# Three first expert passes in plain float32, the first interleaved with the last unit, in a fused scan, feed-forward and routing kernel

## Chip, cores and metric

The kernel runs on one core of one Trainium2 chip. The metric is the device time of one execution in microseconds (us), lower is better. The engines are PE (TensorE, matrix products), ACT (ScalarE), DVE (VectorE), POOL (GpSimd) and SP (SyncE, which here only issues transfers). Each executes its instructions in the order in which they were written.

## What is computed

Three stages follow one another; 3,072 tokens have 256 channels each.

```python
# 1: a chunked scan per head gives x of 3072 x 256
# 2: a feed-forward layer with a rational activation
h = x @ w_in                                   # 256 -> 2048
P = a[0] + a[1]*h + a[2]*h**2 + a[3]*h**3
Q = 1 + abs(b[0])*abs(h) + abs(b[1])*h**2
x = (P / (Q + 1e-6)) @ w_out                   # 2048 -> 256
# 3: each token goes to one of 8 experts
logits = normalized(x) @ normalized(expert_emb).T / tau
e = argmax(logits); gate = softmax(logits)[e]
out = gate * (relu(x @ w1[e]) @ w2[e])         # 256 -> 1024 -> 256
```

## The kernel before

All work is written into a planner (class `Plan`): every instruction has an engine, an estimated duration and a key `at`, and `Plan.run` simulates the engines and starts, on each free engine, the ready instruction with the lowest key. The order so found is the order of the instructions on each engine's queue. Buffers with the same tag (SBUF tiles and PSUM banks) are given out strictly in the order of the first key of their users. Keys count blocks of stage 2: block i of unit u has the key 16u + i.

Stages 1 and 2 run together in six units of 512 tokens, each of 16 blocks of 128 hidden channels (`block`). A block has six products on PE into a bank of four (tag `h`, L735), then five ACT instructions (L740, L741, L742, L746, L747), four on DVE (L744, L749, L750, L751), one on POOL (L752, `gl`), and six products on PE into the unit's two accumulator banks (`acc`, L761). Values on both sides of a product are split into a high and a low float32r part, and three float32r products stand for one float32 product. Unit 5, the last, has no stage 1 beside it.

After a unit, `unit_out` (L773) brings the accumulators to SBUF as x2T, and `route` transposes the rows and computes logits (L794, L796, copies L799 into `row`), finds the expert and the slot in a chain of small DVE instructions (L813 to L850) with one small product (`rk`), and scatters the rows into the table `xs` by four indirect transfers on POOL (L853). After unit 4, `rank` sorts the eight experts by their tokens so far (L873 to L889) and loads the eight numbers into registers of SP (L892), so that the weights of "the expert of rank r" can be fetched.

Stage 3 is a list of passes (rank, first tile, tiles of 128 tokens). FIRST, `(0, 0, [2])` and `(1, 0, [2])`, needs only the tokens of units 0 to 4; THEN needs unit 5's too. Each change of expert loads eight pieces of 256 KB, four of w1 and four of w2 (L941, raw buffers of tag `raw`, four of them), which `weights` splits: high part on ACT (L942), low part by a subtraction on DVE or POOL (L945), into tags `eah`, `eal`, `ebh`, `ebl` with six buffers each. `tokens` fetches rows from `xs` (L956), transposes them (L964) and splits them (L967, L970); `gate` computes the factor (L985 to L1003); `hidden` has six products (L1018) into an `h` bank, a relu split in two (L1020, L1021) and three products for each tile (L1027) into banks of tag `acc`; `deliver` scales (L1041, L1043) and scatters the rows to the output (L1047, POOL). The pool of the fetched rows opens only when all of unit 5's first products are issued (`open_sp`); the pool `w3` of the weights takes the memory of stage 1 (`open_w3`).

Of the kernel before, what the change touches and what calls it, by code (L numbers as in the profile page):

```python
# [17 lines left out]
P = 128  # L18
# [8 lines left out]
TPE = 4  # L27
# [1 line left out]
ROW = DM + NE + 1  # L29


FIRST = [(0, 0, [2]), (1, 0, [2])]
THEN = [(0, 2, [2]), (1, 2, [2])] + [(r, 0, [3]) for r in range(4, NE)] + [(2, 0, [4]), (3, 0, [2, 2])]

WIDE = 4
LATE = 1

SOON = 0.0
EARLY = sum(FIRST[0][2])
assert all(f == (r, 0, [EARLY]) for r, f in enumerate(FIRST))  # L40

# [11 lines left out]
def sh(at, late, early):  # L53

    return at + (early if at < 4 else late)
# [16 lines left out]
class Plan:  # L72
# [29 lines left out]
    def op(self, eng, us, at, fn, r=(), w=(), lag=0.0, size=0, after=(), port=None):  # L102

        port = {None: ("POOL",), True: ("POOL", "DVE"), False: ()}[port]
        o = dict(port=port, on=eng if isinstance(eng, dict) else {eng: us}, any=isinstance(eng, dict), at=at, fn=fn, lag=lag, size=size, i=len(self.ops))
        deps = set()  # L110
        vals = {}
        for x, wr in [(x, False) for x in r] + [(x, True) for x in w]:
            v, s = x if isinstance(x, tuple) else (x, None)
            vals[id(v)] = v
            hit = lambda z: z[1] is None or s is None or z[1] == s
            deps.update(z[0] for z in v.wr if hit(z))
            if wr:
                deps.update(z[0] for z in v.rd if hit(z))
        for x, wr in [(x, False) for x in r] + [(x, True) for x in w]:
            v, s = x if isinstance(x, tuple) else (x, None)  # L120
            if wr:
                if s is None:
# [150 lines left out]
def ssm_ffn_moe_kernel(  # L273
# [54 lines left out]
    def big(shape, dt, name):  # L328
        return plan.val(blk, shape, dt, name, "big", BIG)
# [533 lines left out]
    def rank(s):  # L863

        l0 = (NG - LATE) * BU // P
        v = lambda shape, k, dt=F32: plan.val(blk, shape, dt, f"r{k}", f"r{k}", 1)
        sm, key, rk8, se = v([P, NE], "sm", BF16), v([P, NE], "key"), v([P, NE], "rk8"), v([P, NE, NE], "se")
        cn = bank("cn")
        rows_, cols_ = (lambda ap: ap[:, :, None].to_broadcast([P, NE, NE])), (lambda ap: ap[:, None, :].to_broadcast([P, NE, NE]))

        def f():
            with nc.allow_low_precision(reason="whole numbers below 256"):
                V.tensor_reduce(out=sm.t, in_=oh[:, 0:l0].rearrange("p c e -> p e c"), op=ALU.add, axis=AX.X)  # L873
        dv = lambda us, fn, r, w: op("DVE", us, s, fn, r=r, w=w)
        dv(0.08 + l0 * NE / 960, f, [(oh, u) for u in range(NG - LATE)], [sm])
        op("PE", 0.06, s, lambda: T.matmul(out=cn[:, 0:NE], lhsT=ones.t, rhs=sm.t, start=True, stop=True), r=[ones, sm], w=[cn])

        dv(0.1, lambda: V.scalar_tensor_tensor(out=key.t, in0=cn[:, 0:NE], scalar=float(NE), in1=cw8.t, op0=ALU.mult, op1=ALU.add), [cn, cw8], [key])
        dv(0.15, lambda: V.tensor_tensor(out=se.t, in0=cols_(key), in1=rows_(key), op=ALU.is_gt), [key], [se])
        dv(0.15, lambda: V.tensor_reduce(out=rk8.t, in_=se.t, op=ALU.add, axis=AX.X), [se], [rk8])  # L880

        dv(0.08, lambda: V.tensor_scalar(out=kmin.t, in0=rk8.t, scalar1=float(len(FIRST)), scalar2=float(EARLY * P), op0=ALU.is_lt, op1=ALU.mult), [rk8], [kmin])
        dv(0.08, lambda: V.tensor_scalar(out=tcap.t, in0=rk8.t, scalar1=float(WIDE), scalar2=float(TPE - 1), op0=ALU.is_lt, op1=ALU.add), [rk8], [tcap])

        dv(0.08, lambda: V.tensor_scalar(out=rk8.t, in0=rk8.t, scalar1=-1.0, scalar2=float(NE), op0=ALU.mult, op1=ALU.add), [rk8], [rk8])
        dv(0.15, lambda: V.tensor_tensor(out=se.t, in0=cols_(rk8), in1=rows_(cw8), op=ALU.is_equal), [rk8, cw8], [se])
        dv(0.15, lambda: V.tensor_tensor(out=se.t, in0=se.t, in1=cols_(cw8), op=ALU.mult), [se, cw8], [se])
        dv(0.15, lambda: V.tensor_reduce(out=key.t, in_=se.t, op=ALU.add, axis=AX.X), [se], [key])
        dv(0.08, lambda: V.tensor_scalar(out=slot.t, in0=key.t, scalar1=-1.0, scalar2=float(NE), op0=ALU.mult, op1=ALU.add), [key], [slot])  # L889

        def f():
            _, e = nc.values_load_multi_w_load_instructions(slot[0:1, :], engines=[mybir.EngineType.SP], min_val=0, max_val=NE - 1)  # L892
            expert.extend(e)
        op("SP", 1.0, s, f, r=[slot], w=[ranked])


    def s1_unit(u, lo, hi):
# [32 lines left out]
    def weights(e, i, at, nm):  # L930

        half, q = i % 2, i // 2
        k = "ab"[half]
        shape = [P, 2, 256]
        raw = plan.val(w3, shape, F32, f"r{k}{nm}_{q}", "raw", 4)
        hi, lo = (plan.val(w3, shape, FR, f"e{k}{z}{nm}_{q}", f"e{k}{z}", 6) for z in "hl")
        if half == 0:
            src = lambda: w1[bass.ds(expert[e], 1), :, q * 256:(q + 1) * 256].rearrange("o (k p) f -> p (o k) f", p=P)
        else:
            src = lambda: w2[bass.ds(expert[e], 1), q * 256:(q + 1) * 256, :].rearrange("o (k p) d -> p (o k) d", p=P)  # L940
        op("SP", 0.47, sh(at - 6, -0.52, 0), lambda: D(out=raw.t, in_=src()), r=[one, ranked], w=[raw], size=262144)  # L941
        op("ACT", acts(512), sh(at, 1.69, 0), lambda: A.activation(out=hi.t, in_=raw.t, func=AF.Copy), r=[raw], w=[hi])  # L942
        op(
            {"DVE": dve(512), "POOL": pool2(512)}, 0, sh(at, 7.77, 0),
            lambda g: (G if g == "POOL" else V).tensor_tensor(out=lo.t, in0=raw.t, in1=hi.t.bitcast(F32), op=ALU.subtract),  # L945
            r=[raw, hi], w=[lo], port=True,
        )
        ew[e, k, q] = hi, lo
# [104 lines left out]
    def run_pass(e, t0, parts, at):  # L1053
# [5 lines left out]
        for n in parts:  # L1059
# [15 lines left out]
    for u in range(NBU):  # L1075
        if u + 1 < NBU:
            for v in range(2):
                s1_unit(2 * u + 2 + v, NF * u + 8 * v - 0.5, NF * u + 8 * v + 6.0)
        for i in range(NF):
            block(u, i, NF * u + i)  # L1080
            if u == 0 and i % 2:
                clear(i // 2, 8.0 + i, [last_of[u, i]])
        unit_out(u, NF * (u + 1) + 2 - (SOON if u >= NG - LATE else 0))
        if u < NG - LATE:
            route(u, NF * (u + 1) + 2)
        if u == NG - LATE - 1:
            rank(NF * (u + 1) + 4)
    op("X", 0.0, sh(S3 - 12, 4.15, 0), open_w3, w=[one], after=plan.users(s1p))
    op("X", 0.0, S3 - 2, open_sp, w=[two], after=plan.users(wi))
    at = S3  # L1090
    held = None
    for j, (e, t0, parts) in enumerate(FIRST + THEN):
        if j == len(FIRST):
            for g in range(NG - LATE, NG):
                route(g, NF * (g + 1) + 2)
            at += 4
        if e != held:
            for i in range(8):
# [318 lines left out]
```

## Time and profile before

| | |
|---|---|
| median of 3 runs | 615.38 us (614.1 to 615.79) |
| the profiled execution | 620.6 us, of it the span from first to last instruction 618.8 us |
| PE busy | 551.9 us (89% of the span) |
| DVE busy | 485.5 us (78%) |
| ACT busy | 481.2 us (78%) |
| POOL busy | 258.3 us (42%) |
| granted TensorE clock, mean | 0.957 of full speed |

Shares are means over the span; the stages have different limits, so the rows below are by stretch. Matmuls are pipelined and their durations overlap in the records: what a product costs in a dense stretch is the distance from one start to the next.

### The profile page before, as it was taken

To read this page: it belongs to the slowest core of one execution; us is meant where nothing else is said; L and a number is where in the kernel's file an instruction comes from. 1 tells how busy PE (TensorE), PEld (TensorE's weight loads), DVE (VectorE), ACT (ScalarE), POOL (GpSimd) and SP (SyncE) were. 2 spreads that over 40 slices of the span, in tenths; PEclk is the share of its full clock that TensorE was granted. 3 is DMA by queue.
4 is the path that set the end of the run, shared out by engine and by line. 5 is a ranking of instruction groups with operands and counts; after the bars stand their busy time and mean duration, and the time that the engine had idled before them with its cause. 6 is when DMAs were issued, how large, how long until landed. Compare 5 with 4: busy or idle time off the path is not lost.

```text
span 618.8 us, 10551 instructions
## 1 busy us (share of the span) xinstructions
PE 551.9 (89%) x3477; PEld 428.3 (69%) x3477; DVE 485.5 (78%) x990; ACT 481.2 (78%) x967; POOL 258.3 (42%) x240
## 2 busy tenths in 40 slices
PE   1578989999999999999999998558989999999991
PEld 0144757676676677767766786346979989998991
DVE  7998899899887999899879889477577777766430
ACT  6899989999997999989979997766677656565320
POOL 2573434445445444454454336852456230212111
PEclk9858999999999999999999999768999999999997
DMA  7960606022102110210020012431676655552000
GB/s 249 391 186 19 184 19 183 4 80 73 37 17 93 39 44 32 82 36 1 1 71 2 0 37 86 137 86 35 190 228 188 193 144 155 180 176 76 18 29 14
DMA packets 45728, 58.99 MB, mean 95 GB/s; under 512 B 3991, under 2 KB 35584, under 8 KB 45664
## 3 DMA queue, kind: packets, MB, share of 16 engines
q1 hardware_dynamic: 43168, 51.82, 27.7%
q0 software_dynamic: 2496, 6.41, 2.9%
q8 instruction: 29, 0.48, 0.3%
q14 instruction: 35, 0.29, 0.2%
HBM read 44.02 MB, written 14.72 MB: 95 GB/s over the span
## 4 chain that ended last, share of the span: by engine, by line
PE 55%; issue 13%; DVE 7%; ACT 6%; DMA 5%; POOL 4%; SPq 1%; another core or an unknown queue 0%; POOLq 0%; ACTq 0%
PE acc L761 19%; PE h L735 19%; PE eh L1018 4%; PE y L1027 3%; PE c L663 3%; PE y L703 2%; DMA ra<-in_w 2%; POOL out_dram L1047 2%; PE y L709 2%; PE tk L796 1%; DMA g<-xs 1%; ACT p L740 1%; ACT v L746 1%; DVE u L750 1%; PE st L685 1%
## 5 line engine op out<-in xcount | busy, mean ns | idle before, releaser
L752 POOL TENSOR_TENSOR gl<-p,v 128x512 fp32r<-128x512 f32 x96 | 128.0, 1335 | 169.8 <-DVE p L751 75.8
L735 PE MATMUL h<-x1h,wiw 128*128 128x512 f32 x384 | 144.7, 421 | 19.6 <-DVE p L751 17.3
L761 PE MATMUL acc<-gh,wow 128*128 128x512 f32 x384 | 113.0, 417 | 0.0
L735 PEld LDWEIGHTS h<-x1h,wiw 128*128 128x128 f32 x384 | 75.2, 196 | 47.1 <-DVE p L751 19.6
L761 PEld LDWEIGHTS acc<-gh,wow 128*128 128x128 f32 x384 | 69.6, 193 | 30.1 <-issue 15.9
L749 DVE SCALAR_TENSOR_TENSOR gh<-h,as,v 128x512 fp32r<-128x512 f32 x96 | 71.7, 747 | 21.5 <-ACT v L747 18.8
L744 DVE SCALAR_TENSOR_TENSOR h<-p,sl,h 128x512 f32<-128x512 f32 x96 | 71.8, 749 | 13.1 <-ACT v L741 12.8
L750 DVE SCALAR_TENSOR_TENSOR u<-u,lq,gh 128x512 f32<-128x512 f32 x96 | 80.4, 838 | 0.8
L735 PE MATMUL h<-x1l,wiw 128*128 128x512 f32 x192 | 78.5, 409 | 0.0
L740 ACT ACTIVATE p<-h,kk 128x512 f32<-128x512 f32 x96 | 65.2, 679 | 16.2 <-POOL gl L752 11.3
L751 DVE SCALAR_TENSOR_TENSOR p<-h,as,u 128x512 f32<-128x512 f32 x96 | 71.4, 744 | 3.1 <-issue 0.2
L742 ACT ACTIVATE u<-v,qb 128x512 f32<-128x512 f32 x96 | 69.6, 725 | 1.6
L746 ACT ACTIVATE v<-u,lq 128x512 f32<-128x512 f32 x96 | 69.4, 723 | 1.6
L1027 PE MATMUL y<-ebh,hh 128*128 128x256 f32 x224 | 65.0, 290 | 1.5 <-DVE yo L1043 0.8
L1027 PE MATMUL y<-ebh,hl 128*128 128x256 f32 x224 | 64.1, 286 | 1.9 <-DVE hl L1021 1.5
L1021 DVE SCALAR_TENSOR_TENSOR hl<-eh,hh 128x256 fp32r<-128x256 f32 (+2 forms) x88 | 42.8, 492 | 28.4 <-ACT hh L1020 27.6
L1027 PE MATMUL y<-ebl,hh 128*128 128x256 f32 x224 | 63.3, 282 | 0.0
L1047 POOL DMA_INDIRECT out_dram<-yo,g x28 | 29.0, 1036 | 81.2 <-DVE yo L1043 62.3
L761 PE MATMUL acc<-gl,wow 128*128 128x512 f32 x192 | 61.2, 400 | 1.3 <-POOL gl L752 1.2
L747 ACT ACTIVATE v<-v 128x512 f32<-128x512 f32 x96 | 60.4, 630 | 1.0
L1020 ACT ACTIVATE hh<-eh 128x256 fp32r<-128x256 f32 (+2 forms) x88 | 38.1, 435 | 26.8 <-PE eh L1018 23.9
L741 ACT ACTIVATE v<-h 128x512 f32<-128x512 f32 x96 | 56.9, 593 | 2.5 <-POOL gl L752 2.5
(222 smaller groups left out, 1138.8 us busy)
## 6 DMA issues: line engine op xcount, KB each, us to landing
ra<-in_w SPq DMA_DIRECT2D x40, 256.0 KB
rb<-in_w SPq DMA_DIRECT2D x40, 256.0 KB
xb<-in_xb SPq DMA_DIRECT2D x12, 384.0 KB
xs<-empty SPq DMA_DIRECT2D x8, 530.0 KB
wiwr<-in_w_in SPq DMA_DIRECT2D x8, 512.0 KB
wowr<-in_w_out SPq DMA_DIRECT2D x8, 512.0 KB
xrow<-row SPq DMA_DIRECT2D x6, 530.0 KB
bc<-in_bct SPq DMA_DIRECT2D x12, 256.0 KB
```

What stands on the lines that cost most here:

```text
L735: T.matmul(out=h.t, lhsT=part(wiw[g_], z)[:, k, fs], rhs=xx[:, k, :], start=(k == 0 and e == 0), stop=(k == 1 and e == 2))
L740: op("ACT", act(512, 1), s, lambda: A.activation(out=pp.t, in_=h.t, func=AF.Square, bias=kk.t), r=[h, kk], w=[pp])
L742: op("ACT", acts(512) + 0.06, s + 0.3, lambda: A.activation(out=uu.t, in_=vv.t, func=AF.Square, bias=qb.t), r=[vv, qb], w=[uu])
L744: op("DVE", dve(512, 1), s + 0.8, lambda: stt(out=h.t, in0=pp.t, scalar=sl.t, in1=h.t, op0=ALU.add, op1=ALU.mult), r=[h, pp, sl], w=[h])
L746: op("ACT", acts(512) + 0.09, s + 0.9, lambda: A.activation(out=vv.t, in_=uu.t, func=AF.Ln, bias=lq.t), r=[uu, lq], w=[vv])
L747: op("ACT", acts(512), s + 1.0, lambda: A.activation(out=vv.t, in_=vv.t, func=AF.Exp, scale=-1.0), r=[vv], w=[vv])
L749: op("DVE", dve(512, 1), s + 1.5, lambda: stt(out=gh.t, in0=h.t, scalar=as_.t, in1=vv.t, op0=ALU.add, op1=ALU.mult), r=[h, as_, vv], w=[gh])
L750: op("DVE", dve(512, 1), s + 1.6, lambda: stt(out=uu.t, in0=uu.t, scalar=lq.t, in1=gh.t.bitcast(F32), op0=ALU.add, op1=ALU.mult), r=[uu, l ...
L751: op("DVE", dve(512, 1), s + 1.7, lambda: stt(out=pp.t, in0=h.t, scalar=as_.t, in1=uu.t, op0=ALU.add, op1=ALU.subtract), r=[h, as_, uu], w ...
L752: op("POOL", pool2(512), s + 2.1, lambda: G.tensor_tensor(out=gl.t, in0=pp.t, in1=vv.t, op=ALU.mult), r=[pp, vv], w=[gl])
L761: T.matmul(out=acc[dh].t, lhsT=part(wow[g_], z)[:, i % 2, dh * P:(dh + 1) * P], rhs=x.t, skip_group_check=True, start=(i == 0 and e == 0), ...
L1027: T.matmul(out=y[t // 2][:, t % 2 * DM:(t % 2 + 1) * DM], lhsT=hx[:, o], rhs=wb[w][:, f % 2, :], start=(f == 0 and i == 0 and t % 2 == 0), ...
```

## The change

FIRST becomes three passes, of the experts of ranks 0, 1 and 2; rank 2's pass of four tiles in THEN shrinks to its last two. A new function `first_pass` does them with plain float32 products: the eight weight pieces land unsplit in the `eah`, `eal`, `ebh`, `ebl` buffers, the rows in a `raw` buffer (widened from 512 to 530 words), the transposes go through one bank, the relu is one instruction on ACT or DVE, and one product stands where three float32r products stood. The first of them (`SMALL = 1`) has keys from 92 in steps of 1.2, so it lies among unit 5's last blocks, and its output bank is one of the two small `s` banks; the others follow at key 99 with output in an `acc` bank. Unit 4's `unit_out`, `route` and `rank` get keys that are lower by `AHEAD = 4`; `open_w3` gets key 80; the planner's estimate of the register load is 2.0 in place of 1.0.

```diff
-FIRST = [(0, 0, [2]), (1, 0, [2])]
-THEN = [(0, 2, [2]), (1, 2, [2])] + [(r, 0, [3]) for r in range(4, NE)] + [(2, 0, [4]), (3, 0, [2, 2])]
+FIRST = [(0, 0, [2]), (1, 0, [2]), (2, 0, [2])]
+THEN = [(0, 2, [2]), (1, 2, [2]), (2, 2, [2])] + [(r, 0, [3]) for r in range(4, NE)] + [(3, 0, [2, 2])]
+AHEAD = 4.0
+SMALL = 1
@@ route
+        elif u == NG - LATE - 1:
+            s -= AHEAD
@@ rank
-        op("SP", 1.0, s, f, r=[slot], w=[ranked])
+        op("SP", 2.0, s, f, r=[slot], w=[ranked])
@@ weights
-        raw = plan.val(w3, shape, F32, f"r{k}{nm}_{q}", "raw", 4)
+        raw = plan.val(w3, [P, 2, ROW], F32, f"r{k}{nm}_{q}", "raw", 4)
@@ new
+    def first_pass(e, n, load, at, step, small):
...
+            w = wt[half, q] = plan.val(w3, [P, 2, 256], F32, f"f{k}{nm}_{q}", f"e{k}{'hl'[q % 2]}", 6)
+            op("SP", 0.47, load + 0.1 * i, lambda half=half, q=q, w=w: D(out=w.t, in_=src_of(e, half, q)), r=[one, ranked], w=[w], size=262144)
+        g = plan.val(w3, [P, 2, ROW], F32, f"fg{nm}", "raw", 4)
+        x = plan.val(w3, [P, 2, n * P], F32, f"fx{nm}", "hl", 3)
...
+        tr = bank(f"ft{nm}")
...
+        op("ACT", act(2 * n * P), at - 1.5, lambda: A.activation(out=x.t.rearrange("p k t -> p (k t)"), in_=tr[:, 0:2 * n * P], func=AF.Copy), r=[tr], w=[x])
+        gt = gate(plan, nm, g, n, at + 4 * step, blk)
+        y = bank(f"fy{nm}") if small else plan.val(ps_a, [P, 512], F32, f"fy{nm}", "acc", 2, True)
+        m = n * P
+        for c in range(8):
...
+                for k in range(2):
+                    T.matmul(out=h[:, 0:m], lhsT=wa[:, k, c % 2 * P:(c % 2 + 1) * P], rhs=x[:, k, :], start=(k == 0), stop=(k == 1))
...
+                for t in range(n):
+                    T.matmul(
+                        out=y[:, t * DM:(t + 1) * DM], lhsT=hh[:, t * P:(t + 1) * P], rhs=wb[:, c % 2, :],
...
+            ac = at + step * c
+            op("PE", 0.45 * n, ac - 1, mm1, r=[x, wa], w=[h])
+            op({"ACT": act(m), "DVE": dve(m)}, 0, ac - 18.4, relu, r=[h], w=[hh])
+            op("PE", 0.45 * n, ac + 0.8, mm2, r=[hh, wb], w=[y])
+        deliver(nm, 0, n, g, [y], gt, at + 8 * step + 0.9)
@@ the main list
-        unit_out(u, NF * (u + 1) + 2 - (SOON if u >= NG - LATE else 0))
+        unit_out(u, NF * (u + 1) + 2 - (SOON if u >= NG - LATE else AHEAD if u == NG - LATE - 1 else 0))
-            rank(NF * (u + 1) + 4)
-    op("X", 0.0, sh(S3 - 12, 4.15, 0), open_w3, w=[one], after=plan.users(s1p))
+            rank(NF * (u + 1) + 4 - AHEAD)
+    op("X", 0.0, NF * (NG - 1), open_w3, w=[one], after=plan.users(s1p))
+        if j < len(FIRST):
+            first_pass(e, EARLY, NF * (NG - 1) + 2 + 2 * j, 92.0 if j < SMALL else at, 1.2 if j < SMALL else 0.5, j < SMALL)
+            at += 2 * EARLY if j >= SMALL else 0
+            continue
```

## Rows read from the trace of the kernel before

**Rows 1.** The page's 40 equal slices of the span: busy tenths of PE

```profile
PE   1578989999999999999999998558989999999991
```

**Rows 2.** Busy time by stretch: length, then PE, PEld, DVE, ACT, POOL, clock, DMA

```profile
377.60:391.80 14.20, 10.89 (x43) 7.60 (x42) 11.63 (x16) 10.56 (x20) 8.95 (x8) 1.00 0.32 104
391.80:416.00 24.20, 11.47 (x30) 8.73 (x30) 13.17 (x17) 16.24 (x29) 19.15 (x15) 0.65 0.47 131
416.00:429.40 13.40, 10.48 (x43) 8.21 (x42) 11.74 (x36) 7.93 (x24) 4.18 (x3) 0.87 0.13 41
429.40:459.20 29.80, 27.92 (x230) 26.30 (x228) 17.19 (x49) 19.81 (x53) 12.79 (x11) 1.00 0.62 183
459.20:606.20 147.00, 143.13 (x1051) 138.77 (x1051) 93.94 (x251) 82.01 (x217) 37.44 (x34) 1.00 0.43 129
```

**Rows 3.** Timeline of PE: start, us, instruction, idle before it and what ended it

```profile
398.07 0.80 PE L735 MATMUL h<-x1h,wiw 128*128 128x512 f32 x1 [6.25 <-DVE p L751]
409.30 0.80 PE L735 MATMUL h<-x1h,wiw 128*128 128x512 f32 x1 [6.48 <-DVE p L751]
```

**Rows 4.** Timeline of ACT

```profile
370.97 0.67 ACT L740 ACTIVATE p<-h,kk 128x512 f32<-128x512 f32 x1
374.07 0.67 ACT L740 ACTIVATE p<-h,kk 128x512 f32<-128x512 f32 x1
381.49 0.69 ACT L740 ACTIVATE p<-h,kk 128x512 f32<-128x512 f32 x1 [3.57 <-POOL gl L752]
410.70 0.69 ACT L740 ACTIVATE p<-h,kk 128x512 f32<-128x512 f32 x1 [4.67 <-POOL gl L752]
429.41 1.27 ACT L773 ACTIVATE x2T<-acc,fin 128x512 f32<-128x512 f32 x2 [1.45 <-PE acc L761]
```

**Rows 5.** Groups of 377.6 to 429.4, shapes apart: busy us, mean ns, idle before

```profile
L945 POOL TENSOR_TENSOR eal<-ra,eah 128x512 fp32r<-128x512 f32 x6 | 8.0, 1349 | 0.3 <-ACT eah L942 0.3
L942 ACT ACTIVATE eah<-ra 128x512 fp32r<-128x512 f32 x6 | 3.8, 632 | 1.6 <-DMA ra<-in_w 1.4
L1020 ACT ACTIVATE hh<-eh 128x256 fp32r<-128x256 f32 x1 | 0.4, 383 | 0.6 <-PE eh L1018 0.6
```

**Rows 6.** Timelines of DVE and SP: routing chain, ranks, first weight piece fetched

```profile
366.67 0.18 DVE L813 TENSOR_REDUCE mx<-row 128x4 f32<-128x32 f32 x1
379.44 0.16 DVE L889 TENSOR_SCALAR slot<-rkey 128x8 int32<-128x8 f32 x1
...
382.93 0.40 SPq L941 DMA_DIRECT2D ra<-in_w  x1
```

**Rows 7.** Busy time of L735, then L761, in unit 5's rest

```profile
377.60:429.40 51.80, 12.86 (x37) 8.38 (x36) 0.80 0.34 100
377.60:429.40 51.80, 19.70 (x66) 14.29 (x66) 0.80 0.34 100
```

**Rows 8.** Chain that ended last, dense runs of products: start, us to next piece

```profile
367.30 1.40 PE acc L761 x6
431.95 0.35 PE tk L796 x4
435.74 0.71 PE eh L1018 x6
436.44 0.72 PE y L1027 x6
```

**Rows 9.** Weight loads of a plain float32 product, 512 columns on the moving side

```profile
321.84 0.29 PEld L663 LDWEIGHTS c<-cz,bc 64*128 64x128 f32 x2 [0.36 <-issue]
322.73 0.29 PEld L663 LDWEIGHTS c<-cz,bc 64*128 64x128 f32 x2 [0.59 <-DVE x1l L720]
```

**Rows 10.** From unit 5's end to THEN: rows fetched (SP, chain), first product (PE)

```profile
450.09 4.71 DMA g<-xs
459.25 0.39 PE L1018 MATMUL eh<-xl,eah 128*128 128x256 f32 x1 [0.37 <-DVE xl L970]
```

**Rows 11.** Waits of SP's queue from 380 to 606: total, times, longest

```profile
SPq L941 <- DVE eal L945: 29.2, 11, 14.9
```

More of the change, by code (lines that the diff above doesn't have):

```diff
@@ L940, in weights @@
             src = lambda: w2[bass.ds(expert[e], 1), q * 256:(q + 1) * 256, :].rearrange("o (k p) d -> p (o k) d", p=P)
-        op("SP", 0.47, sh(at - 6, -0.52, 0), lambda: D(out=raw.t, in_=src()), r=[one, ranked], w=[raw], size=262144)
-        op("ACT", acts(512), sh(at, 1.69, 0), lambda: A.activation(out=hi.t, in_=raw.t, func=AF.Copy), r=[raw], w=[hi])
+        op("SP", 0.47, sh(at - 6, -0.52, 0), lambda: D(out=raw[:, :, 0:256], in_=src()), r=[one, ranked], w=[raw], size=262144)
+        op("ACT", acts(512), sh(at, 1.69, 0), lambda: A.activation(out=hi.t, in_=raw[:, :, 0:256], func=AF.Copy), r=[raw], w=[hi])
         op(
             {"DVE": dve(512), "POOL": pool2(512)}, 0, sh(at, 7.77, 0),
-            lambda g: (G if g == "POOL" else V).tensor_tensor(out=lo.t, in0=raw.t, in1=hi.t.bitcast(F32), op=ALU.subtract),
+            lambda g: (G if g == "POOL" else V).tensor_tensor(out=lo.t, in0=raw[:, :, 0:256], in1=hi.t.bitcast(F32), op=ALU.subtract),
             r=[raw, hi], w=[lo], port=True,
@@ L1066, in run_pass, with src_of, f, mm1 @@
             q += n
+    def src_of(e, half, q):
+        if half == 0:
+            return w1[bass.ds(expert[e], 1), :, q * 256:(q + 1) * 256].rearrange("o (k p) f -> p (o k) f", p=P)
+        return w2[bass.ds(expert[e], 1), q * 256:(q + 1) * 256, :].rearrange("o (k p) d -> p (o k) d", p=P)
+    def first_pass(e, n, load, at, step, small):
+        nm = f"{e}_0"
+        wt = {}
+        for i in range(8):
+            half, q = i % 2, i // 2
+            k = "ab"[half]
+            w = wt[half, q] = plan.val(w3, [P, 2, 256], F32, f"f{k}{nm}_{q}", f"e{k}{'hl'[q % 2]}", 6)
+            op("SP", 0.47, load + 0.1 * i, lambda half=half, q=q, w=w: D(out=w.t, in_=src_of(e, half, q)), r=[one, ranked], w=[w], size=262144)
+        g = plan.val(w3, [P, 2, ROW], F32, f"fg{nm}", "raw", 4)
+        x = plan.val(w3, [P, 2, n * P], F32, f"fx{nm}", "hl", 3)
+        op("SP", 0.47, load - 0.1, lambda: D(out=g.t, in_=xs[bass.ds(expert[e] * CAP, n * P), :].rearrange("(t p) c -> p t c", p=P)), r=[xs_v, xs_c, one, ranked], w=[g], size=n * P * ROW * 4)
+        tr = bank(f"ft{nm}")
+        def f():
+            for t in range(n):
+                for k in range(2):
+                    T.transpose(out=tr[:, (k * n + t) * P:(k * n + t + 1) * P], in_=g[:, t, k * P:(k + 1) * P], identity=ident.t)
+        op("PE", 0.22 * n, at - 1.5, f, r=[g, ident], w=[tr])
+        op("ACT", act(2 * n * P), at - 1.5, lambda: A.activation(out=x.t.rearrange("p k t -> p (k t)"), in_=tr[:, 0:2 * n * P], func=AF.Copy), r=[tr], w=[x])
[3 more added lines that the diff above has]
+        for c in range(8):
+            h = plan.val(ps_h, [P, 512], F32, f"fh{nm}_{c}", "h", H_B, True)
+            hh = plan.val(w3, [P, TPE * P], F32, f"fr{nm}_{c}", "hh", 3)
+            wa, wb = wt[0, c // 2], wt[1, c // 2]
+            def mm1(h=h, wa=wa, c=c):
+                for k in range(2):
+                    T.matmul(out=h[:, 0:m], lhsT=wa[:, k, c % 2 * P:(c % 2 + 1) * P], rhs=x[:, k, :], start=(k == 0), stop=(k == 1))
+            def relu(eng, h=h, hh=hh):
+                if eng == "ACT":
+                    A.activation(out=hh[:, 0:m], in_=h[:, 0:m], func=AF.Relu)
+                else:
+                    V.tensor_scalar(out=hh[:, 0:m], in0=h[:, 0:m], scalar1=0.0, scalar2=None, op0=ALU.max)
+            def mm2(hh=hh, wb=wb, c=c):
+                for t in range(n):
+                    T.matmul(
+                        out=y[:, t * DM:(t + 1) * DM], lhsT=hh[:, t * P:(t + 1) * P], rhs=wb[:, c % 2, :],
+                        start=(c == 0 and t == 0), stop=(c == 7), skip_group_check=True,
+                    )
+            ac = at + step * c
[3 more added lines that the diff above has]
+        deliver(nm, 0, n, g, [y], gt, at + 8 * step + 0.9)
```

## Prediction

> **What bounds the kernel now.** I read the page's slices first. PE is busy nine tenths or more nearly everywhere, and there is one hole, four slices (8, 5, 5, 8) from 371 to 433 us [rows 1]. So the end is set by PE's work plus what PE loses, and the loss sits where stage 2 hands over to stage 3. The windows by stretch put numbers on it [rows 2]. From 391.8 to 416.0 PE is busy 11.47 of 24.20 us at a mean granted clock of 0.65, so part of that work ran at the lower level, 1.2 GHz, and took double; from 459.2 to 606.2 it is busy 143.13 of 147.00 at full clock. After 606.2 there are 12.6 us of tail that the change does not touch.
>
> What makes the hole: PE stands for 6.25 and 6.48 us before two first products of unit 5's blocks, which lack a free bank because the DVE work of earlier blocks is late [rows 3]. DVE was late for ACT, and ACT for POOL: ACT idles 4.67 us for `gl` before the block at 410.70 [rows 4]. POOL was splitting the weights of the first expert at 1349 ns a piece (six of `eal`, as many of `ebl`), in order ahead of unit 5's `gl`; ACT splits six pieces of each kind too, at 632 ns, and waited there for the transfers [rows 5]. So the first pass's preparation, not its products, held unit 5 up. Unit 5 ends with x2T at 429.41 [rows 4]; from there its routing has to reach `xs` and come back: rows fetched at 450.09, landed 4.71 later, first product of THEN at 459.25 [rows 10]. PE fills that time with both first passes.
>
> **The books of before, from 377.6 us.** Work at full clock: unit 5 has 37 and 66 products left, that is 17 groups of six [rows 7], at 1.40 a group [rows 8] 23.9 us. A split first pass has 8 chunks of six products into `eh` and six into `y`, 0.71 and 0.72 a group [rows 8]: 11.4, two of them 22.9, with 0.9 for their transposes (eight at about 0.11). Unit 5's routing on PE I put at 2.5 (four tiles; the logits are 0.35 each [rows 8], the transposes and the small products the rest). THEN is 143.1 [rows 2]. Sum 193.3, so PE would be done at 570.9; it is done at 606.2. The 35.3 lost are 26.7 until 429.4 (51.8 less 25.1 of work), 4.7 from 429.4 to 459.2 and 3.9 after it.
>
> **Products in plain float32.** For what one costs, the scan's own plain product with 512 moving columns: it appears as two instructions, and the next one's weight loads start 0.89 later [rows 9]. That row has 64 rows of weights, the new products 128; the distance is what 1,024 columns for each of the two instructions would need at the 1.40 for six times 512 of [rows 8] (0.93), so I take half of 0.89, 0.445, for 256 columns; the ends are 0.43 and 0.47. A chunk has two products into `h` and two into `y`: 1.78; a pass 14.2 in place of 11.4. Three passes: 42.7, with transposes 1.4. THEN loses two tiles of one pass: a tile is eight chunks of half of 1.43, 5.7, with transposes 5.9, so 11.8 less: 131.3. PE's work is 23.9 + 42.7 + 1.4 + 2.5 + 131.3 = 201.8, 8.5 more than before, and PE would be done at 579.4.
>
> The Trainium skill says in "TensorE: Matmul & The Clock Gate", Part 3, The mechanism, that a weight load overlaps running matmuls only where the row group differs, which would not hold here. The trace speaks against it: a float32r pair of a 128-column load and 256 moving columns takes 0.118 a piece, half of the 0.233 for 512 columns [rows 8], so the load hides. The cost in time of the rule, were it so for plain products, is a rival below.
>
> **What the change takes away.** The splits of two first experts leave ACT and POOL (16 pieces each kind of work). In unit 5 that frees POOL's 15 us and the ACT waits, so neither 6 us wait has its cause any more. What then sets unit 5's end is ACT: one block in 3.10 us (370.97 to 374.07 [rows 4]), against 2.8 on PE. ACT first loses 3.57 us at 381.49 to `gl`, which waits for POOL's scatters of unit 4 [rows 4]; that stays, and with it PE's 3.3 idle until 391.8 [rows 2]. From 381.5 eight blocks are 24.8; the first pass adds on ACT its copy (0.6), squares and small functions of the gate (1.8) and half of eight relus at 0.38 [rows 5], 3.9 in all. ACT is done at 410.2; the last block's DVE, POOL and PE steps take some 4 more, so x2T starts at about 415 in place of 429.4. Until then PE has 23.9 of blocks, 3.3 idle, and room for 10 of the first pass's 14.2: the fit is tight but holds. After 415: 4 left of it, 28.4 and 0.9 for the other two passes, 2.5 of routing, and the same 4.7 of bubbles: 455.5. The rows of THEN, by the old distance of 29.8 from x2T to first product [rows 4, 10], are ready at 445, so PE and not the routing is last. Then 131.3 + 3.9 idle: PE done at 590.7.
>
> **What the change adds in waits.** The first pass's products, its copy and its squares stand in order on PE and ACT among unit 5's blocks, and wait there for transfers. Behind them wait the blocks' products on PE and `p` and `v` on ACT, and all of unit 5's end waits for those. The ranks: the chain runs from 366.67 to 379.44, about one small DVE instruction between two of the blocks', and the first fetch goes out 3.5 us later [rows 6]. Lower keys can't shorten the alternation; they save the wait for rows and transposes ahead of it, 2 to 3 us, and the scatters, fetch and SP's register loads move with it. The fetch needs up to 4.7 to land [rows 10], so the first product can start at about 388. The planner's estimate is short of that by some 3 us (its 2.0 against 3.5 and a quicker landing). I charge 3; the ends are 0 (the backlog in four banks covers it) and 13 (both old waits again, [rows 3]). The 24 pieces and three fetches on SP at about 0.6 each keep its queue for 16 us with nothing else due. A third short pass in THEN, with eight pieces to fetch and split in 11.4 us, costs 1.5 (0 to 4). The third expert's second load is hidden by the three-tile passes' slack. The output bank in `s` leaves one bank for the routing of unit 5 only while the first pass lasts, about 4 us of PE work past x2T: at worst 3 us on a chain with 10 us of slack, nothing.
>
> Sum: 590.7 + 3 + 1.5 = 595.2, against 606.2: 11.0 us less. The profiled execution, 620.6, would be 609.6. It is 0.85% above the median; the same 11 off the median, 615.4, gives 604.4, and I say 604.
>
> **Rivals.**
> *Late transfers* (0.17). The first pass waits in the order as the splits did; of the 13 us about 7 to 10 more than I charged come back: 611 to 615, middle 612. For it: the order is laid out by a planner that was 6 us off here before. Against: four banks of blocks stand ahead of the wait.
> *It is not interleaved* (0.06). Ranks come no sooner and the first pass runs wholly after unit 5. Then x2T is at 412 and PE has 14.2 + 28.4 + 1.4 + 2.5 + 4.7 to do: THEN at 463, done at 600: 609.
> *Raw buffers* (0.13), slower. The three first passes hold three of the four `raw` buffers until they are delivered, and THEN's weight pieces all pass through what is left, behind one queue, SP, whose weight loads already wait up to 14.9 us for a subtraction [rows 11]. A piece needs about 6.5 (fetch 4, split 0.63 and 0.7 to 1.35, queues): one buffer from 397 to 420, two to 437, three after, is some 8 pieces by 436, in time for 455. It decides from about 10 us a piece: then the first two THEN experts are 10 and 15 us late, and the time is 617 to 625.
> *Loads that do not hide* (0.03), slower. One 128-column load is 0.0875 (0.35 for four short products, [rows 8]); 64 in a pass, three passes: 16.8, so 621. This is what the page's rule above would do.
> *Better* (0.02): all waits zero, bubbles halved: below 597.5.
>
> **How the numbers follow.** My forecast has 0.59: 604, with 598 to 611. A measurement here can tell about 0.3%, 1.85 us. Faster takes 0.59 + 0.06 + 0.02 and 0.11 of the late transfers (up to 613.5): 0.78. Same: 0.06, the rest of them. Slower: 0.13 + 0.03. The range 597 to 617 holds the forecast, the missing interleave and the late transfers, 0.82; it leaves out the slower rivals and the best case.
>
> **What the profile after should show.** Right: no PE wait over 4 us between 380 and 420; x2T of unit 5 at 412 to 420; four plain products of a chunk in 1.7 to 1.9; THEN's first product at 452 to 460 with PE busy up to it; PE done near 595. Wrong: x2T after 424 means the transfers; x2T early but holes in PE after 450 before products that wait for ACT or DVE splits means the buffers; chunks over 2.2 the loads; chunks of the first pass all after x2T, no interleave. The prediction also fails if ACT, with copies and gates in unit 5, gets slower than 3.6 a block.

## The result, and the profile after

The kernel after takes 608.58 us in the median (607.9 to 609.87). The kernel before took 615.59 us beside it, so the ratio is 0.9889 [0.9858, 0.9919], or 7.0 us less. I predicted 11.0 less and 604 us. The sign was right and the time lies in the range, but over a third of the gain that I worked out isn't there.

The profiled executions (620.6 before, 609.87 after) differ by 10.7 us, and 3.65 of that arises ahead of the change: the same instruction, x2T of unit 4, starts at 358.47 in one and at 354.82 in the other. Experiments whose instructions stand in the same order up to that point show either value, so this part belongs to the execution and not to the change. Everything below is therefore counted from x2T of unit 4. The two rows are from ACT's timelines (start, duration, instruction), first before, then after:

```profile
358.47 1.26 ACT L773 ACTIVATE x2T<-acc,fin 128x512 f32<-128x512 f32 x2
```

```profile
354.82 1.26 ACT L776 ACTIVATE x2T<-acc,fin 128x512 f32<-128x512 f32 x2
414.21 1.27 ACT L776 ACTIVATE x2T<-acc,fin 128x512 f32<-128x512 f32 x2 [1.50 <-PE acc L764]
```

| us after unit 4's x2T | before | predicted | after |
|---|---|---|---|
| x2T of unit 5 | 70.9 | 59.5, with the charge of 3 | 59.4 |
| THEN's first product | 100.8 | 100.0 | 101.1 |
| PE done | 247.7 | 236.7 | 240.8 |

From the page of after, the 40 slices for PE and its clock, which stand against [rows 1]:

```profile
PE   1567989999999999999999999899979979999991
PEclk9868999999999999999999999999999989999996
```

And windows of after (length, then PE, PEld, DVE, ACT, POOL, clock, DMA), cut as in [rows 2]:

```profile
391.80:416.00 24.20, 23.21 (x105) 18.86 (x104) 18.91 (x53) 17.73 (x44) 10.84 (x8) 1.00 0.57 179
...
429.40:459.20 29.80, 26.57 (x126) 22.30 (x125) 18.71 (x68) 12.61 (x39) 10.39 (x10) 0.94 0.48 153
459.20:596.00 136.80, 130.49 (x987) 128.85 (x985) 86.39 (x212) 75.08 (x196) 36.01 (x32) 0.99 0.43 131
```

The hole of unit 5 is gone. In 391.8 to 416.0 PE is busy 23.21 us at full clock, where it had 11.47 at 0.65, and POOL falls from 19.15 to 10.84. What is new is smaller and lies later: two slices of 7 among nines (441 to 456 and 486 to 502 us), a clock of 0.94 before 459.2, and 5.9 us idle from there to PE's last product (595.63), where before had 3.9.

**The first pass lies where it should.** PE's timeline of after: its first and last products around x2T (414.21), and then three steps of a later pass:

```profile
388.70 1.10 PE L1108 MATMUL fh<-fx,fa 128*128 128x256 f32 x4
394.71 1.03 PE L1118 MATMUL fy<-fb,fr 128*128 128x256 f32 x4
414.25 1.89 PE L1108 MATMUL fh<-fx,fa 128*128 128x256 f32 x8
...
438.00 1.03 PE L1108 MATMUL fh<-fx,fa 128*128 128x256 f32 x4
438.86 1.03 PE L1118 MATMUL fy<-fb,fr 128*128 128x256 f32 x4
439.73 1.03 PE L1108 MATMUL fh<-fx,fa 128*128 128x256 f32 x4
```

A row of "x4" is two products of two instructions each. Six of the eight `fh` steps and five of the eight `fy` steps were done by x2T; five steps of 0.86, 4.3 us, were left. From 438.00 to 438.86 two products take 0.86 us, so one takes 0.43, a chunk 1.73 and a pass 13.8.

**Two holes are new.** The first is at THEN's start. SP's timeline of after shows the pieces of THEN's weights as their raw buffers come free, then ACT and PE:

```profile
399.39 0.37 SPq L946 DMA_DIRECT2D ra<-in_w  x1
407.93 0.37 SPq L946 DMA_DIRECT2D rb<-in_w  x1
414.87 0.37 SPq L946 DMA_DIRECT2D ra<-in_w  x1
425.01 0.37 SPq L946 DMA_DIRECT2D rb<-in_w  x1
434.54 0.37 SPq L946 DMA_DIRECT2D ra<-in_w  x1
```

```profile
452.77 0.63 ACT L947 ACTIVATE eah<-ra 128x512 fp32r<-128x512 f32 x1 [1.16 <-DMA ra<-in_w]
453.31 0.37 ACT L972 ACTIVATE xh<-t 128x256 fp32r<-128x256 f32 x1
```

```profile
454.84 0.24 PE L1180 MATMUL ck<-oh,ones 128*128 128x8 bf16 x4 [2.05 <-DVE xl L975]
454.94 1.58 PE L1118 MATMUL fy<-fb,fr 128*128 128x256 f32 x4
455.96 0.78 PE L1023 MATMUL eh<-xh,eah 128*128 128x256 f32 x1
456.53 0.41 PE L1023 MATMUL eh<-xl,eah 128*128 128x256 f32 x1
456.75 0.41 PE L1023 MATMUL eh<-xh,eal 128*128 128x256 f32 x1
```

Five pieces go out in 35 us, and the rest have to follow in a bunch from 442.59. So ACT stands at 452.77 for a piece that has not landed, the copy `xh` of THEN's rows queues behind it, `xl` on DVE comes after that, and PE waits 2.05 us (`ck` takes the small bank that `xl` gives back). Then PE runs at the lower of its two levels, 1.2 GHz (0.55 granted on the mean from 456.0 to 459.2): the products come 0.21 us apart where 0.118 is the distance at full clock, until about 458.9.

The second is inside THEN. DVE's, POOL's and PE's timelines of after:

```profile
489.15 3.13 DVE L1000 TENSOR_SCALAR sq<-sq 128x3 f32<-128x3 f32 x1
```

```profile
488.35 1.39 POOL L1052 DMA_INDIRECT out_dram<-yo,g  x1 [0.30 <-DVE sq L999]
489.76 1.28 POOL L950 TENSOR_TENSOR eal<-ra,eah 128x512 fp32r<-128x512 f32 x1
490.98 1.27 POOL L950 TENSOR_TENSOR ebl<-rb,ebh 128x512 fp32r<-128x512 f32 x1
```

```profile
493.43 0.69 PE L969 MATMUL t<-ident,g 128*128 128x128 f32 x2 [3.49 <-DVE xl L975]
495.20 0.41 PE L1023 MATMUL eh<-xh,eah 128*128 128x256 f32 x1
495.41 0.41 PE L1023 MATMUL eh<-xl,eah 128*128 128x256 f32 x1
```

A DVE instruction on three numbers a partition, 0.16 to 0.18 us elsewhere, lasts 3.13. It ends when POOL's three instructions in a row end (490.98 + 1.27 = 492.25). Behind it on DVE stood the `xl` that PE waited 3.49 us for, and after that wait PE again ran at the lower level, 0.21 us a product.

### The profile page after: what moved, and what is told of

Read it like the earlier page. It is cut to its first block, busy times and chain, and to the rows that moved or that the text cites. A ratio compares the mean times of both kernels' runs of the same rounds, so it can differ in the third digit from the quotient of the medians.

```text
span 608.1 us, 10413 instructions
## 1 busy us (share of the span) xinstructions
PE 550.6 (91%) x3429; PEld 428.0 (70%) x3429; DVE 485.2 (80%) x994; ACT 467.4 (77%) x940; POOL 243.9 (40%) x229
## 4 chain that ended last, share of the span: by engine, by line
PE 53%; issue 14%; DVE 8%; DMA 7%; POOL 4%; ACT 3%; SPq 1%; POOLq 0%; DVEq 0%; ACTq 0%
PE acc L764 19%; PE h L738 19%; PE c L666 3%; DMA g<-xs 3%; PE y L706 2%; POOL out_dram L1052 2%; PE eh L1023 2%; PE fy L1118 1%; PE y L712 1%; PE tk L801 1%; PE y L1032 1%; DVE gh L752 1%; DMA out_dram<-yo,g 1%; DMA fg<-xs 1%; DVE u L753 1%
## 5 line engine op out<-in xcount | busy, mean ns | idle before, releaser
L738 PE MATMUL h<-x1h,wiw 128*128 128x512 f32 x384 | 142.0, 413 | 9.0 <-DVE p L754 5.9
L738 PEld LDWEIGHTS h<-x1h,wiw 128*128 128x128 f32 x384 | 73.7, 192 | 35.3 <-DVE p L754 7.5
L764 PEld LDWEIGHTS acc<-gh,wow 128*128 128x128 f32 x384 | 67.9, 188 | 29.5 <-issue 15.9
L738 PE MATMUL h<-x1l,wiw 128*128 128x512 f32 x192 | 76.9, 401 | 0.0
L750 ACT ACTIVATE v<-v 128x512 f32<-128x512 f32 x96 | 60.4, 629 | 1.0
L1026 DVE SCALAR_TENSOR_TENSOR hl<-eh,hh 128x256 fp32r<-128x256 f32 (+1 forms) x72 | 34.3, 480 | 26.7 <-ACT hh L1025 26.2
L1032 PE MATMUL y<-ebh,hh 128*128 128x256 f32 x176 | 51.2, 291 | 1.3 <-ACT hh L1025 1.3
L1052 POOL DMA_INDIRECT out_dram<-yo,g x22 | 22.9, 1040 | 71.7 <-DVE yo L1048 51.6
L1032 PE MATMUL y<-ebh,hl 128*128 128x256 f32 x176 | 50.4, 286 | 1.1 <-DVE hl L1026 1.1
L1025 ACT ACTIVATE hh<-eh 128x256 fp32r<-128x256 f32 (+1 forms) x72 | 30.4, 424 | 26.0 <-PE eh L1023 23.5
L1032 PE MATMUL y<-ebl,hh 128*128 128x256 f32 x176 | 49.8, 283 | 0.0
```

What stands on the lines that cost most here:

```text
L738: T.matmul(out=h.t, lhsT=part(wiw[g_], z)[:, k, fs], rhs=xx[:, k, :], start=(k == 0 and e == 0), stop=(k == 1 and e == 2))
L750: op("ACT", acts(512), s + 1.0, lambda: A.activation(out=vv.t, in_=vv.t, func=AF.Exp, scale=-1.0), r=[vv], w=[vv])
L764: T.matmul(out=acc[dh].t, lhsT=part(wow[g_], z)[:, i % 2, dh * P:(dh + 1) * P], rhs=x.t, skip_group_check=True, start=(i == 0 and e == 0), ...
L1032: T.matmul(out=y[t // 2][:, t % 2 * DM:(t % 2 + 1) * DM], lhsT=hx[:, o], rhs=wb[w][:, f % 2, :], start=(f == 0 and i == 0 and t % 2 == 0), ...
```

## The experiments

Ratios are to the kernel before on the same chip, with their 95% intervals. The first theory was: the raw buffers, held by the fetched rows of the first passes, cost the missing time. Rivals: the third first pass is too much work, or the low keys and the interleaving don't pay.

**e1_early_release.** The rows' raw buffer is let go sooner: the gate is computed at the pass's start, and the output indices are copied out of the row.

```diff
-        gt = gate(plan, nm, g, n, at + 4 * step, blk)
+        ix = plan.val(w3, [P, 2], I32, f"fi{nm}", "fi", 3)
+        op("DVE", 0.08, at - 1.4, lambda: V.tensor_copy(out=ix.t, in_=g[:, 0:n, ROW - 1].bitcast(I32)), r=[g], w=[ix])
+        gt = gate(plan, nm, g, n, at - 1.4, blk)
...
-        deliver(nm, 0, n, g, [y], gt, at + 8 * step + 0.9)
+        deliver(nm, 0, n, g, [y], gt, at + 8 * step + 0.9, ix)
```

> The changed kernel (608.6 us), with the fetched rows of the three first passes given back early: the index column is copied into a small tile, the gate is computed right after the transposes, so the raw buffer is free some 10 us after the rows land and not when the pass is delivered. Theory (raw buffers: only five weight pieces for THEN are issued between 399 and 435, and THEN's first product waits for the last of them): the pieces are issued sooner, the 2 us wait and the low clock before THEN's first product go, 604 to 606. Rival (the routing of unit 5 sets THEN's start, rows land at 439 to 443): no change, 608 to 609.

Measured: 604.55 us, 0.9846 [0.9813, 0.9879], 3.4 and 4.2 us under e2 and e4 below on the same chip, which stand where the change stands (the intervals still overlap a little). Its windows of the two holes of after, and its THEN (PE's last product ends at 589.81):

```profile
456.00:459.20 3.20, 3.20 (x27) 3.08 (x27) 3.13 (x11) 1.86 (x5) 2.74 (x3) 1.00 0.35 123
490.00:500.00 10.00, 8.79 (x60) 8.59 (x59) 5.29 (x15) 6.61 (x19) 3.57 (x4) 1.00 0.66 197
454.66:590.20 135.54, 131.01 (x1002) 129.17 (x1000) 85.13 (x218) 75.54 (x197) 42.53 (x37) 1.00 0.44 131
```

The same windows of after:

```profile
456.00:459.20 3.20, 3.20 (x17) 3.11 (x16) 3.03 (x12) 0.63 (x2) 2.27 (x2) 0.55 0.36 106
490.00:500.00 10.00, 6.57 (x42) 6.57 (x42) 6.96 (x17) 5.18 (x15) 3.53 (x3) 0.83 0.59 182
```

THEN starts at full clock and takes 135.2 us in place of 139.7. But it does not start sooner: 101.1 us after unit 4's x2T, as in after. The way from unit 5's x2T to THEN is 2.4 us shorter (39.35 for 41.75), while unit 5 itself ends 2.3 later (61.7). So in this run the gain lies in THEN and not ahead of it. As the release also changes the order of everything behind it, it removed the second hole too, and the run can't say how much of the gain is whose; f3 and g2 below say more.

**e2_no_ahead** (the keys), **e3_not_interleaved** (the interleaving) and **e4_two_first** (the third pass) undo one part of the change each:

```diff
-AHEAD = 4.0
+AHEAD = 0.0
```

```diff
-SMALL = 1
+SMALL = 0
```

```diff
-FIRST = [(0, 0, [2]), (1, 0, [2]), (2, 0, [2])]
-THEN = [(0, 2, [2]), (1, 2, [2]), (2, 2, [2])] + [(r, 0, [3]) for r in range(4, NE)] + [(3, 0, [2, 2])]
+FIRST = [(0, 0, [2]), (1, 0, [2])]
+THEN = [(0, 2, [2]), (1, 2, [2])] + [(r, 0, [3]) for r in range(4, NE)] + [(2, 0, [4]), (3, 0, [2, 2])]
```

> The changed kernel with the old keys for unit 4's output, routing and ranks (AHEAD = 0). Theory (the keys save only the 2 to 3 us before the small DVE chain, the chain alternates with the blocks either way): first pass starts 2 to 3 us later, 609 to 611. Rival (sooner ranks are what frees unit 5): 613 to 616, about half of the gain gone or more.

> The changed kernel with all three first passes behind unit 5 (SMALL = 0), output in the accumulator banks. Theory (PE has about 10 us of idle time in unit 5 that the first pass fills): unit 5 ends 1 to 3 us sooner, but THEN starts later, 611 to 614. Rival (the gain is only that nothing is split during unit 5, and the interleaved pass costs the blocks what it saves): 607 to 609.

> The changed kernel with two first passes instead of three; rank 2's pass is again one of four tiles in THEN. Theory (PE's work is the bound, but 14 us of cover behind unit 5 are too little for the 25 us until THEN's rows land): PE idles 8 to 10 us before THEN with the clock falling, PE work is 2.4 us less, a raw buffer more is free: 606 to 611. Rival (the third pass is needed as cover, all of the gain): 613 to 617.

Measured: e2 607.96 us, 0.9899 [0.9867, 0.9931]; e3 612.13, 0.994 [0.9919, 0.9961]; e4 608.75, 0.9892 [0.9863, 0.9921]. The change stands at 0.9889. So the keys and the third pass can't be told from nothing, and the interleaving is worth about half of the gain (the intervals of e3 and of the change just touch). In e3 some `fh` steps still run among unit 5's blocks, but no `fy` does before x2T, and unit 5 ends no sooner for that (61.4 us for 59.4). THEN starts at 106.9.

**f2_keys_only** does the keys alone, on the kernel before (with the estimate of 2.0 and the earlier pool).

```diff
+AHEAD = 4.0
+        elif u == NG - LATE - 1:
+            s -= AHEAD
...
-            rank(NF * (u + 1) + 4)
+            rank(NF * (u + 1) + 4 - AHEAD)
```

> The kernel before with only the changed keys and estimates: AHEAD = 4 for unit 4's output, routing and ranks, 2.0 for the register load, open_w3 at key 80; two split first passes as before. Theory (the split work on POOL and ACT in unit 5 is what holds unit 5 up, and the keys do not bring the ranks sooner): within 2 us of before, 614 to 617. Rival (the planner's late ranks and its short estimate were the cause): 608 to 612.

Measured: 619.29 us, 1.0019 [0.9999, 1.0039]. PE stands for 6.25 and 6.49 us in unit 5, the two waits of [rows 3] as they were.

**f3_no_pool_split** leaves the planner no choice for the subtraction that makes the low part of a weight:

```diff
-            {"DVE": dve(512), "POOL": pool2(512)}, 0, sh(at, 7.77, 0),
+            {"DVE": dve(512)}, 0, sh(at, 7.77, 0),
```

> The changed kernel with the low parts of all weights subtracted on DVE alone, none on POOL. Theory (the 3.5 us hole of PE at 490 comes from a small DVE instruction of the gate that stood 3.1 us while POOL subtracted): that hole goes, 604.5 to 607, less what DVE's extra 0.69 us for each piece costs. Rival (the hole is the late fetch of the fourth pass's rows, landed at 484): the hole stays, 608 to 610.

Measured: 604.27 us, 0.9788 [0.9768, 0.9808], in place of the change's 0.9889. The second hole is gone, and of the small instructions on DVE from 377 to 600 us only one lasts over 1 us (1.22). The first hole stays, since the raw buffers are held as in after; PE's timeline of f3:

```profile
457.06 0.24 PE L1180 MATMUL ck<-oh,ones 128*128 128x8 bf16 x4 [2.67 <-DVE xl L975]
458.65 0.78 PE L1023 MATMUL eh<-xh,eah 128*128 128x256 f32 x1
```

**f4_half_products** is e1 with one of the two `fh` products of each chunk left out in the passes of ranks 1 and 2, 16 products of 0.43 us or 6.9 us of PE.

```diff
-                for k in range(2):
-                    T.matmul(out=h[:, 0:m], lhsT=wa[:, k, c % 2 * P:(c % 2 + 1) * P], rhs=x[:, k, :], start=(k == 0), stop=(k == 1))
+                kk_ = 2 if small else 1
+                for k in range(kk_):
+                    T.matmul(out=h[:, 0:m], lhsT=wa[:, k, c % 2 * P:(c % 2 + 1) * P], rhs=x[:, k, :], start=(k == 0), stop=(k == kk_ - 1))
```

> The kernel with early release (604.6 us), with the second of the two first-layer products left out in the first passes of ranks 1 and 2: their hidden values are wrong, PE has 16 products of 0.43 us less, 6.9 us. Theory (PE's products are the last to be done before THEN, so the plain product's price is on the path): THEN starts 5 to 7 us sooner, 598 to 600. Rival (THEN's rows, landed at about 445, or its weight pieces set the start): 603 to 605.

Measured: 605.7 us, 0.9814 [0.9793, 0.9835]; e1 has 0.9846 [0.9813, 0.9879]. Of 6.9 us of products 2 at most came back, as the rival had it: the intervals overlap. ACT's timeline of f4 shows why:

```profile
419.57 1.27 ACT L776 ACTIVATE x2T<-acc,fin 128x512 f32<-128x512 f32 x2 [1.35 <-PE acc L764]
...
448.29 0.42 ACT L990 ACTIVATE jk<-g 128x256 f32<-128x256 f32 x1 [4.23 <-DMA g<-xs]
```

PE is through with nearly all products of the first passes at 447.9. Then it waits 1.98 and 1.21 us for two last relus on DVE and 0.95 for an `xl`. DVE itself had stood 3.28 us for the rows of THEN, which landed 28.7 us after x2T; THEN's first product comes at 457.21, 37.6 after x2T. So the path of the rows sets the start here, with its last leg in the same queues as gates, relus and splits, and it is only 1.7 us shorter than what e1 takes with all products (39.35).

**f5_gate_port** is e1 with the planner told that the gate's small DVE instructions and POOL exclude one another (`port=True`).

```diff
-        dv = lambda us, fn, r, w: plan.op("DVE", us, sh(at, 0.85, 0), fn, r=r, w=w)
+        dv = lambda us, fn, r, w: plan.op("DVE", us, sh(at, 0.85, 0), fn, r=r, w=w, port=True)
```

> The kernel with early release, with the planner told that the gate's small DVE instructions can't run beside POOL's (port = True). Theory (waits of small DVE instructions for POOL are left in this kernel, at 487 for instance, 1.2 us): 602 to 604.5. Rival (chance of the order): 604 to 608.

Measured: 602.67 us, 0.9774 [0.9742, 0.9805], better than e1 (0.9846 [0.9813, 0.9879], on another chip). But seven DVE instructions on 2 to 24 numbers still last 1.0 us or more, 1.60 at the longest, where e1 has seven of up to 1.22, and none of 3 us stands in either. So the gain is there and my reason for it is not shown: the new order does something else better, and what that is stays open.

**g1_before_no_pool** is f3's edit on the kernel *before*: no plain products, no interleaving, no lower keys. **g2_early_no_pool** is e1 with f3's edit, **g3_two_no_pool** is g2 with e4's lists.

> The kernel before with the low parts of all weights subtracted on DVE alone. Theory (POOL's subtractions held up gl, and with it unit 5): the two waits of 6 us in unit 5 become shorter and the waits of the gate's small instructions go, 603 to 610, though DVE now carries 12 pieces of 0.69 us in unit 5. Rival (the transfers that ACT waits for in order hold unit 5, POOL only follows): unit 5 ends as late as before, 612 to 617.

> The changed kernel with early release of the fetched rows and all subtractions on DVE. Theory (two separate costs, buffers and POOL beside DVE): 600 to 603, below each alone on the same chip. Rival (both edits take away the same holes): as the one with subtractions on DVE alone, 0.979 of before, 603 to 605.

> As the last, with two first passes instead of three. Theory (the third first pass brings nothing, its products are dearer and its cover is not needed): the same time within 1.5 us. Rival (without holes behind, the third pass is needed as cover for the routing of unit 5): 3 to 6 us more.

Measured: g1 606.8 us, 0.9769 [0.975, 0.9788]; g2 604.02, 0.9735 [0.9714, 0.9756]; g3 607.18, 0.9776 [0.975, 0.9802]. One line in the kernel before is thus worth twice the whole change. The window of g1 that answers to the hole, its x2T of units 4 and 5, and its groups of the splits from 377.6 to 430:

```profile
391.80:417.80 26.00, 19.99 (x93) 14.72 (x92) 25.52 (x53) 23.46 (x54) 9.59 (x7) 1.00 0.33 102
```

```profile
359.75 1.26 ACT L773 ACTIVATE x2T<-acc,fin 128x512 f32<-128x512 f32 x2
417.82 1.26 ACT L773 ACTIVATE x2T<-acc,fin 128x512 f32<-128x512 f32 x2
```

```profile
L945 DVE TENSOR_TENSOR eal<-ra,eah 128x512 fp32r<-128x512 f32 x9 | 6.2, 684 | 2.7 <-ACT eah L942 2.7
L942 ACT ACTIVATE eah<-ra 128x512 fp32r<-128x512 f32 x9 | 5.7, 637 | 3.7 <-DMA ra<-in_w 3.7
```

Unit 5 ends 58.1 us after unit 4's x2T, against 70.9 before and 59.4 after, though ACT still splits nine pieces of `eah` in this stretch, six of them before that x2T. The longest wait of PE in unit 5 is 1.61 us, the clock stays full, and the split first pass begins at 409.74, inside unit 5, with nobody having interleaved it. ACT waits for no transfer before that x2T. So the hole came from POOL's subtractions, and neither ACT's part nor the transfers make it without them.

How they made it is another matter, and not a queue on POOL ahead of `gl`. DVE's and POOL's timelines of the kernel before:

```profile
388.60 0.74 DVE L749 SCALAR_TENSOR_TENSOR gh<-h,as,v 128x512 fp32r<-128x512 f32 x1
391.84 0.75 DVE L749 SCALAR_TENSOR_TENSOR gh<-h,as,v 128x512 fp32r<-128x512 f32 x1 [1.84 <-PE acc L761]
395.63 0.75 DVE L749 SCALAR_TENSOR_TENSOR gh<-h,as,v 128x512 fp32r<-128x512 f32 x1 [2.37 <-ACT v L747]
396.29 0.87 DVE L750 SCALAR_TENSOR_TENSOR u<-u,lq,gh 128x512 f32<-128x512 f32 x1
397.27 0.75 DVE L751 SCALAR_TENSOR_TENSOR p<-h,as,u 128x512 f32<-128x512 f32 x1
```

```profile
399.49 1.28 POOL L752 TENSOR_TENSOR gl<-p,v 128x512 fp32r<-128x512 f32 x1
409.39 2.97 POOL L752 TENSOR_TENSOR gl<-p,v 128x512 fp32r<-128x512 f32 x2 [2.02 <-DVE p L751]
```

On DVE each block has `gh`, then `u`, then `p`, and `p` frees the bank that PE waits for at 398.07 [rows 3]. Here the `u` that belongs to the `gh` of 388.60 stands behind the `gh` of two later blocks, which waited 1.84 us for PE and 2.37 for ACT. Before PE's second wait two such `u` stand behind a `gh` at 405.55. In g1 each `u` starts within 1.4 us of its `gh`. POOL's own queue cost less: the `gl` of 399.49 came 1.5 us after its `p` had ended, and the next one found POOL idle for 2.02 us, waiting for DVE.

The order is the planner's. The kernel marks `u` (L750) `port=True`, like the subtraction, so the planner starts it only while it takes POOL to be free, and twelve subtractions in a row left few such moments. No run changes that mark alone, so this path is read from the order on DVE and from the kernel's text.

With the hole gone the rest of the change is worth little. f3 (the whole change without POOL) stands at 0.9788 and g1 at 0.9769. f3 and g2 differ by the early release alone, and their intervals don't overlap: 0.53 points, on two chips. THEN starts 100.6 us after unit 4's x2T in f3 and 97.1 in g2, so there the buffers cost time ahead of THEN. All in all g2 gains 0.34 points over g1, and of g2 the third pass is 0.41 points (g3 against g2); in both pairs the intervals still overlap by a hair, so neither is settled. g2 is the fastest of its comparison, 2.65% under the kernel before, against 1.1% for the change.

## Why the prediction came out as it did

**The cause of the hole** held in its source, POOL's splits, as g1 shows by itself. The path that I gave, splits "in order ahead of unit 5's `gl`" and "DVE was late for ACT, and ACT for POOL", did not: ACT's 4.67 us for the `gl` of 409.39 lead back to DVE, for which POOL idled, and on DVE `u` stood late in the order. "ACT splits six pieces of each kind too … and waited there for the transfers" named a second cause that is none by itself: in g1 ACT makes the same twelve splits ahead of x2T and unit 5 is as short as after the change.

**The plain product** was 0.43 us, for 0.445 taken from the 512-column product of [rows 9]; the pass 13.8 for 14.2. The loads hide with 128 rows too, and that rival fell: two loads of 0.0875 apiece have no room in 0.43. The rule beside it (the Trainium skill, "TensorE: Matmul & The Clock Gate", Part 3, The mechanism) does not hold for these products.

**Unit 5's end** was predicted at 56.5 us past unit 4's x2T and 59.5 with the charge of 3 for transfers; it came at 59.4. The sum was right by luck: PE waited for no transfer in unit 5. What I had mis-sized is ACT's extra work. I counted one gate, one copy and half of eight relus, 3.9 us; the groups of ACT in after from 377.6 to x2T show three gates, since all three fetches had landed:

```profile
L990 ACT ACTIVATE jk<-fg 128x256 f32<-128x256 f32 x6 | 2.5, 411 | 0.0
L1097 ACT ACTIVATE fx<-ft 128x512 f32<-128x512 f32 x2 | 1.2, 589 | 0.0
L1112 ACT ACTIVATE fr<-fh 128x256 f32<-128x256 f32 x3 | 1.1, 373 | 0.0
L1005 ACT ACTIVATE ex<-ex 128x16 f32<-128x16 f32 x3 | 0.7, 217 | 3.2 <-DVE ex L1004 3.2
```

With the accumulator reads, the other functions of the gates and two splits that is 9.1 us of work, and 3.2 of waiting for DVE's chain. Part of it falls behind the last block, whose last function on ACT ends 53.4 us after unit 4's x2T (408.26) for 51.7 predicted; from there to x2T it takes 6.0 us for 4.8.

**"Lower keys … save 2 to 3 us"** failed. The first fetch goes out 24.7 us after unit 4's x2T (379.54), against 24.5 before (382.93, [rows 6]). f2 and e2 agree: nothing.

**The s bank and "a chain with 10 us of slack"**: the four tiles of unit 5's `tk` are spread from 415.97 to 422.5 where before they stood within 3.2 us, as I had feared. The rows did not land later for it. SP sends three fetches from 435.32, for THEN's first three passes in order, and ACT's timeline shows when the first has landed:

```profile
439.57 0.42 ACT L990 ACTIVATE jk<-g 128x256 f32<-128x256 f32 x1 [1.44 <-DMA g<-xs]
```

That is 25.4 us after x2T, as before ([rows 10] less [rows 4]); the second pass's rows landed at 442.67. So the bank cost nothing. But the slack was not 10: I carried over the old 4.5 us from landing to first product, and in f4, where this path decides, rows land 28.7 us after x2T and that leg takes 8.9. Against e1, which starts THEN 39.35 us after x2T, some 2 us of slack are left.

**THEN's start** was 1.1 us off (101.1 for 100.0), with the wait of 2.05 in it: 4.3 us of the first pass were left at x2T, for 4 predicted. It means that the whole 11.5 us won in unit 5 are spent by then, on the third pass and the dearer products.

**THEN itself** is the step that failed, by 3.0 us: 131.3 of work + 3.9 + 1.5 was 136.7, and it took 139.7. I took over the idle time of the THEN before, in which PE's longest wait was 0.9 us, and gave the third short pass 1.5 us as if it could only be late by itself. In its place stood twelve products at 0.21 us for 0.118 at THEN's start, some 1.1 us, the wait of 3.49, and about 3 us at the lower clock after 493.43, some 1.5 lost. e1 has none of the three and takes 135.2, 1.5 less than my sum. f3, where only the second hole is gone, takes 132.6 (458.65 to 591.29). So it is that hole, the wait beside POOL, that put THEN over the sum; the new orders changed other waits too.

**The raw buffers** were a rival that I had on the other side of zero, "slower" from 10 us a piece. The mechanism acts, with 7 to 10 us between SP's pieces, but it makes two short waits and not two late experts. e1 puts it, with the second hole that went with it, at 3 to 4 us, and g2 against f3, without that hole, at half a point or some 3 us: it takes back a part of the gain and doesn't turn the sign. My error was to give it a price only from the point where it turns the sign. The "should show" line had it right: x2T early and a wait in PE after 450 for a DVE split means the buffers.

**Not interleaved** was put at 609 and measured as 0.994, or 612: there the freed unit 5 is not filled, as the rival said, and the unit ends no sooner, as it did not say.

## What to carry over

When an engine that is lightly loaded on the average (POOL, 42%) stands in a chain of short stages, move the foreign work off it before restructuring anything: here one line did twice what the whole change did. When an engine waits, look at the order of its own queue before blaming the engine it waits for: here instructions that could have run stood behind later ones. Price a stage that follows a change with its own queues, buffers and order, and not with the idle time that it showed before. And let go of a shared buffer at its last real use: an index and a factor, a few numbers a row, held three of four weight buffers here.

## What the hardware showed that I had not expected

**A tiny DVE instruction can wait for POOL, and longer than one POOL instruction.** On 128x3 numbers `TENSOR_SCALAR` took 3.13 us in after and 3.14 in e2, beside a scatter and two subtractions on POOL back to back; in kernels with no subtraction on POOL (f3, g1) the longest was 1.22 us, in g2 none reached 0.95. The Trainium skill, "SBUF — State Buffer", Who interferes with whom, says that DVE and GpSimd share a pair of ports, that a `tensor_scalar` can enter a mode that uses it, and that whoever issues first keeps it for the whole instruction. The row agrees in kind. By that rule the wait would have ended with the first POOL instruction, at 489.74; the trace shows that it ended with the third, at 492.25. A large instruction does the same: in the kernel before a `u` (L750, 128x512) lasted 3.71 us from 379.55, for 0.75 elsewhere, beside a scatter and two `gl` that ended at 382.70.

**The subtraction that POOL does in 1.27 to 1.35 us takes DVE 0.68** (g1's groups, [rows 5]), so on the busier engine (DVE 78% of the span, POOL 42%) it takes half the time. In g1 DVE is busy 25.5 of the 26.0 us from 391.8 to 417.8, and unit 5 still ends 12.9 us sooner than before.
